# Making the w1 operands of an expert's last group one group earlier, and the gate's Sinkhorn iteration on 128 partitions at fixed places among the products

## The chip, the cores and the metric

The kernel runs on one core of a Trainium2 chip. The metric is the device time of one execution in microseconds (us). A core has five engines that run side by side, each working through its own queue in order: TensorE (PE, matrix products; the load of their stationary operand is shown apart, as PEld), VectorE (DVE), ScalarE (ACT), GpSimd (POOL) and SyncE (SP, which here issues all DMAs). They wait for each other by semaphores. L12 is line 12 of the kernel.

## The reference

```python
attn_out = _attn_ref(**attn_kwargs)            # delta-rule attention, 4 x 8 heads, 768 steps
x = attn_out.transpose(0, 2, 1, 3).reshape(B * S, H * D)      # 3072 tokens x 384
x = _moe_ref(x=x, **moe_kwargs)                # leaky ReLU layer, 384 -> 2048 -> 384
# _moe2_ref
logits = x @ w_gate                            # 3072 x 8
P = np.exp(logits - logits.max())
for _ in range(8):                             # Sinkhorn iteration
    P /= P.sum(1, keepdims=True) + 1e-09
    P /= P.sum(0, keepdims=True) + 1e-09
    P *= N / E
for e in range(E):                             # 8 experts, 384 -> 1024 -> 384
    out += P[:, e:e + 1] * (np.maximum(x @ w1[e], 0.0) @ w2[e])
```

## The kernel before, in words

The program has two parts. Up to about 905 us it computes the attention with the first layer among it, and writes that layer's result x to DRAM. From there to the end it computes the eight experts, and only this second part is touched. Float32 products are made on PE as three passes of split operands: every operand is held as a high part and a low remainder (names ending in h and l), and a product is high x high, high x low and low x high.

**The experts.** The tokens are taken in three blocks p of 1024; for each block the eight experts e run one after the other, 24 in all. An expert has four groups k = 0 to 3 (the list `groups`, L707), and each group makes two of the eight 128-wide slices of the hidden layer. The products of a group follow a Strassen-like scheme of 11 terms (class Group, L894 to L952, in the written order first, second, third, fourth, fifth); each term is three matmuls of 512 columns, issued by `prod` (L872). `second` and `fourth` of a group are issued inside the next group, so that PE always has work. After the fourth group come the products with w2: `second(ps, ...)` (L954) for eight blocks of 128 tokens, eight slices f each, three matmuls of 384 columns per slice; `flush` (L962) adds the block to the accumulator, with the gate's weights pm from expert 1 on, and by a plain ACT copy for expert 0.

**The weights.** `load_w1` and `load_w2` fetch the raw weights of one group by DMA into one of two staging buffers (tile stg, L683). `make_w1(n)` (L727) forms four sums on POOL (L731), then the high part of nine blocks in two ACT instructions (L733, three blocks and six blocks) and the low part in two POOL instructions (L734); `make_w2` is one ACT instruction (L744) and one on POOL (L745). w1 operands live in a ring of three (`w1o[n % 3]`), w2 operands in a ring of five. The queue `prep` (class Stage, L748) holds the tasks: `prep.now()` makes the task at its head and fetches the next loads, so that at most two are staged. The main loop (L981) fills it at k = 0 of each expert and calls `weights()` once per group, inside `fifth` (L949), that is before the group's last three matmuls; three more tasks are made in blocks 1, 3 and 5 of the w2 stage. In the kernel before the order is:

- k = 0: w2 of group n+1; k = 1: w2 of n+2; k = 2: w2 of n+3, then w1 of n+3; k = 3: w2 of n+4
- blocks 1, 3, 5: w1 of n+4, n+5, n+6

Here n is the expert's first group. So w1 of the fourth group (n+3) is made at the end of the third, right before the fourth needs it.

**The order on the engines.** A scheduler orders the instructions of each engine by its own estimate of times. `ordered` (L711) overrides it: it chains an instruction to the one passed to it before on the same engine, so that these keep the written order. Matmuls of the products, the ACT copies and the DVE additions of a group, and the ACT part of the weights are ordered; POOL's instructions, the DMAs, and before the change all of the gate's work are not.

**The gate.** `gate_block` (L564) multiplies 512 tokens with w_gate (six matmuls with 32 stationary columns), transposes on DVE and adds into `logits`, which has 32 partitions x 96 groups x 8 experts. The first five blocks of tokens are done in the first part; the sixth is loaded late (`late_x`, L863, ACT and DVE, not ordered) into tiles of hidden slices 5 to 7, which are free until group 2 of expert 0 writes them. `sinkhorn` (L820) is a generator: each `yield` gives control back until the next call of `bgq.pump`. Before the change `pump` is called once per `prod` and once per block of the w2 stage. It takes the maximum, the exponential, eight iterations of nine DVE instructions with one small matmul (L850, the sum over partitions), and at the end four DMAs (L858) that spread the result over 128 partitions as `pm`. Expert 1's first `flush` needs pm.

Of the kernel before, what the change touches and what calls it, by code (L numbers as in the profile page):

```python
# [8 lines left out]
F32 = mybir.dt.float32  # L9
# [5 lines left out]
ALU = mybir.AluOpType  # L15
# [34 lines left out]
def delta_moe_kernel(ctx: ExitStack, tc: tile.TileContext, k_l, v_l, q_l, beta_l, wa_in, wg, wc, out):  # L50
# [510 lines left out]
            sp.dma_start(out=x2_dram[t, c], in_=o)  # L561


    def gate_block(xh, xl, t, ps_fn, lt):  # L564
        ps = ps_fn()
        for i, x in enumerate((xh, xl)):
            for c in range(KD):
                pe.matmul(out=ps[0:32], lhsT=wg_r[:, c], rhs=x[c] if isinstance(x, list) else x[:, c], start=(i == 0 and c == 0),
                          stop=(i == 1 and c == KD - 1))
            yield  # L570
        dve.transpose(out=lt.rearrange("p g e -> p (g e)"), in_=ps[0:32])
        dve.tensor_tensor(out=logits[:, t * TB // 32:(t + 1) * TB // 32], in0=lt[:, :, 0:E], in1=lt[:, :, E:2 * E],
                          op=ALU.add)
        yield

    if True:
# [238 lines left out]
        def misc(name):  # L815
            return ms_p.tile([128, 512], F32, tag="ms", name=name)

        G = N // 32

        def sinkhorn():  # L820
            yield from gate_block(*g5, NT - 1, lambda: misc("gate"), lt)
            mx = acc_p.tile([32, 1], F32, name="mx")
            dve.tensor_reduce(out=mx, in_=logits, axis=AX.XY, op=ALU.max)
            yield
            ps = misc("mx_ps")
            pe.transpose(out=ps[0:1, 0:32], in_=mx, identity=ident[0:32, 0:32])
            m1 = acc_p.tile([1, 1], F32, name="m1")
            dve.tensor_reduce(out=m1, in_=ps[0:1, 0:32], axis=AX.X, op=ALU.max)
            yield
            ps = misc("mb_ps")  # L830
            pe.matmul(out=ps[0:32, 0:1], lhsT=ones[0:1, 0:32], rhs=m1, start=True, stop=True)
            dve.tensor_copy(out=mx, in_=ps[0:32, 0:1])
            dve.tensor_scalar(out=logits, in0=logits, scalar1=mx, scalar2=None, op0=ALU.subtract)
            p32 = acc_p.tile([32, G, E], F32, name="p32")
            act.activation(out=p32, in_=logits, func=ACTF.Exp)
            yield
            rs = acc_p.tile([32, G], F32, name="rs")
            cs = acc_p.tile([32, E], F32, name="cs")
            for _ in range(8):
                dve.tensor_reduce(out=rs, in_=p32, axis=AX.X, op=ALU.add)  # L840
                dve.tensor_scalar(out=rs, in0=rs, scalar1=1e-9, scalar2=None, op0=ALU.add)
                dve.reciprocal(out=rs, in_=rs)
                dve.tensor_tensor(out=p32, in0=p32, in1=rs.unsqueeze(2).to_broadcast([32, G, E]), op=ALU.mult)
                yield
                dve.tensor_reduce(out=cs, in_=p32.rearrange("p g e -> p e g"), axis=AX.X, op=ALU.add)
                yield
                yield
                yield
                ps = misc("cs_ps")
                pe.matmul(out=ps[0:32, 0:E], lhsT=ones[0:32, 0:32], rhs=cs, start=True, stop=True)  # L850
                yield
                dve.tensor_scalar(out=cs, in0=ps[0:32, 0:E], scalar1=1e-9, scalar2=None, op0=ALU.add)
                dve.reciprocal(out=cs, in_=cs)
                dve.tensor_tensor(out=p32, in0=p32, in1=cs.unsqueeze(1).to_broadcast([32, G, E]), op=ALU.mult)
                dve.tensor_scalar(out=p32, in0=p32, scalar1=float(N // E), scalar2=None, op0=ALU.mult)
                yield
            for k in range(4):
                sp.dma_start(out=pm[32 * k:32 * k + 32], in_=p32.rearrange("p (n k) e -> p k n e", k=4)[:, k])  # L858
            yield

        g5 = [[hb[5 + c][1][i] for c in range(KD)] for i in range(2)]

# [91 lines left out]
        def second(ps, n, blk, fs):  # L954
            o = blk % 4 * 128
            for f in fs:
                w2 = [x[:, f % 2] for x in w2o[(n - n % 4 + f // 2) % W2R]]
                for i, (wt, xx) in enumerate(passes(w2, hb[f][blk // 4])):
                    ordered(pe.matmul(out=ps[:, 0:DM], lhsT=xx[:, o:o + 128], rhs=wt, start=(f == 0 and i == 0),  # L959
                                      stop=(f == NF2 - 1 and i == 2), skip_group_check=True))  # L960

        def flush(ps, p, e, blk):  # L962
            y, a = ps[:, 0:DM], acc[:, blk]
# [12 lines left out]
        def add_w(load, make, n):  # L976
            if n < len(groups):
                prep.add(load, make, n)

        prev = None  # L980
        for n, (p, e, k) in enumerate(groups):  # L981
            g = Group(n)
            if k == 0:
                xs = [2 * p + 2, 2 * p + 3] if e == E - 1 and p < NT // 2 - 1 else []
                for j in range(1, 4):
                    add_w(load_w2, make_w2, n + j)
                add_w(load_w1, make_w1, n + 3)
# [24 lines left out]
            g.hi(0, 1)  # L1012
            second(ps[0], n, 0, range(NF2 - 2))
            g.second()
            g.lo(0, 1)
            g.hi(1, 0)
            g.lo(1, 0)
            second(ps[1], n, 1, range(NF2 - 2))
            g.fourth()
            g.hi(1, 1)  # L1020
            g.lo(1, 1)
            edge = e == E - 1 and p < NT // 2 - 1
            for blk in range(2 * B):
# [12 lines left out]
_OUT = ((N, DM), "float32")  # L1036
# [42 lines left out]
```

## Time and profile before

| | |
|---|---|
| median of 3 runs | 2592.79 us (2587.26 to 2599.87) |
| the profiled execution | 2577.62 us |
| its span, first to last instruction | 2575.9 us |
| mean granted TensorE clock | 0.957 of full speed |
| PE busy | 2401.5 us, 93% of the span |
| PEld, DVE, ACT, POOL busy | 81%, 51%, 45%, 37% |
| the expert part | from about 905 us to the end, 24 experts |

The profile shows one execution. Each row of a timeline gives the start in us from the span's beginning, the length, the engine, the line, the operation and its tiles; in brackets stands how long the engine was idle before it and what released it. A matmul's shown length overlaps the next one, so the distance of two starts is what it costs: about 0.23 us for 512 columns and 0.18 us for 384 at the full clock.

### The profile page before, as it was taken

To read this page: it belongs to the slowest core of one execution; us is meant where nothing else is said; L and a number is where in the kernel's file an instruction comes from. 1 tells how busy PE (TensorE), PEld (TensorE's weight loads), DVE (VectorE), ACT (ScalarE), POOL (GpSimd) and SP (SyncE) were. 2 spreads that over 40 slices of the span, in tenths; PEclk is the share of its full clock that TensorE was granted. 3 is DMA by queue.
4 is the path that set the end of the run, shared out by engine and by line. 5 is a ranking of instruction groups with operands and counts; after the bars stand their busy time and mean duration, and the time that the engine had idled before them with its cause. 6 is when DMAs were issued, how large, how long until landed. Compare 5 with 4: busy or idle time off the path is not lost.

```text
span 2575.9 us, 35446 instructions
## 1 busy us (share of the span) xinstructions
PE 2401.5 (93%) x13836; PEld 2094.3 (81%) x13836; DVE 1302.0 (51%) x2320; ACT 1163.9 (45%) x2121; POOL 964.0 (37%) x966
## 2 busy tenths in 40 slices
PE   6888899999999978999999999999999999999999
PEld 5776778777877767898888888888888888888888
DVE  8667747364622578444444544444444534444443
ACT  6888565756554443333333443333333433333332
POOL 6435211323322223434444444443333434334441
PEclk7678999999999999999999999999999999999999
DMA  3355633333344521111111311111111211111111
GB/s 119 128 171 188 210 130 111 129 103 128 111 150 145 198 68 39 44 49 44 49 44 49 95 48 54 50 44 49 38 49 49 92 50 43 44 49 43 50 43 37
DMA packets 108695, 214.83 MB, mean 83 GB/s; under 512 B 11504, under 2 KB 79728, under 8 KB 108528
## 3 DMA queue, kind: packets, MB, share of 16 engines
q1 hardware_dynamic: 108528, 212.58, 26.4%
q8 instruction: 108, 1.77, 0.3%
q14 instruction: 59, 0.48, 0.1%
HBM read 190.43 MB, written 22.02 MB: 82 GB/s over the span
## 4 chain that ended last, share of the span: by engine, by line
PE 72%; ACT 9%; DVE 7%; issue 5%; POOL 4%; DMA 2%; POOLq 0%; SPq 0%; ACTq 0%; DVEq 0%
PE ye L959 31%; PE ph L875 12%; PE y L875 6%; PE z L875 5%; PE w L875 4%; PE ph L503 4%; PE po L555 4%; ACT x L271 2%; PE y_ps L346 1%; PE w_ps L337 1%; ACT a_d L205 1%; POOL w1l L734 1%; DMA stg<-wc 1%; DVE tm L237 1%; ACT p L287 1%
## 5 line engine op out<-in xcount | busy, mean ns | idle before, releaser
L745 POOL TENSOR_TENSOR w2l<-stg,w2h 128x768 fp32r<-128x768 f32 x96 | 181.6, 1891 | 671.2 <-ACT w2h L744 671.2
L731 POOL TENSOR_TENSOR stg<-stg 128x128 f32<-128x128 f32 x384 | 235.3, 633 | 300.8 <-DMA stg<-wc 293.3
L971 DVE SCALAR_TENSOR_TENSOR acc<-ye,pm,acc 128x384 f32<-128x384 f32 x168 | 103.5, 616 | 437.4 <-PE ye L959 437.4
L734 POOL TENSOR_TENSOR w1l<-stg,w1h 128x384 fp32r<-128x384 f32 x192 | 271.3, 1437 | 56.2 <-ACT w1h L733 35.8
L885 ACT ACTIVATE xc<-ph 128x512 f32<-128x512 f32 x96 | 57.5, 599 | 510.8 <-PE ph L875 408.9
L875 PE MATMUL ph<-xoh,w1l 128*128 128x512 f32 x480 | 197.1, 411 | 42.3 <-POOL w1l L734 42.3
L555 PE MATMUL po<-gh,w 128*128 128x512 f32 (+1 forms) x600 | 215.0, 402 | 2.9 <-ACT gh L543 2.7
L875 PE MATMUL ph<-xoh,w1h 128*128 128x512 f32 x480 | 194.2, 405 | 17.9 <-ACT w1h L733 6.4
L890 DVE TENSOR_TENSOR q<-q,ph 128x512 f32<-128x512 f32 x192 | 131.8, 687 | 119.4 <-PE ph L875 119.4
L875 PE MATMUL ph<-xol,w1h 128*128 128x512 f32 x480 | 188.4, 392 | 0.0
L503 PE MATMUL ph<-x1h,w 128*128 128x512 f32 (+1 forms) x600 | 181.8, 409 | 6.5 <-DVE leak L541 4.0
L733 ACT ACTIVATE w1h<-stg 128x384 fp32r<-128x384 f32 x192 | 121.2, 680 | 117.8 <-DMA stg<-wc 83.7
L890 DVE TENSOR_TENSOR c<-xc,y 128x512 f32<-128x512 f32 x96 | 66.0, 687 | 189.0 <-PE y L875 164.5
L875 PEld LDWEIGHTS ph<-xoh,w1l 128*128 128x128 f32 x480 | 92.6, 193 | 70.9 <-POOL w1l L734 52.3
L541 DVE TENSOR_TENSOR leak<-leak,ph 128x512 f32<-128x512 f32 (+1 forms) x100 | 66.3, 663 | 159.0 <-ACT leak L540 158.6
L875 PEld LDWEIGHTS ph<-xoh,w1h 128*128 128x128 f32 x480 | 93.4, 195 | 51.9 <-ACT w1h L733 16.1
L503 PEld LDWEIGHTS ph<-x1h,w 128*128 128x128 f32 x600 | 110.9, 198 | 29.7 <-DVE leak L541 5.2
L555 PEld LDWEIGHTS po<-gh,w 128*128 128x128 f32 x600 | 113.7, 193 | 25.2 <-ACT gh L543 5.9
L545 POOL TENSOR_TENSOR gl<-leak,gh 128x512 fp32r<-128x512 f32 x48 | 62.1, 1295 | 174.7 <-ACT gh L543 161.8
L555 PE MATMUL po<-gl,w 128*128 128x512 f32 (+1 forms) x300 | 119.4, 399 | 4.7 <-POOL gl L545 3.2
L875 PEld LDWEIGHTS ph<-xol,w1h 128*128 128x128 f32 x480 | 91.0, 190 | 14.9
L540 ACT ACTIVATE leak<-ph 128x512 f32<-128x512 f32 (+1 forms) x100 | 57.8, 578 | 90.0 <-PE ph L503 87.7
(316 smaller groups left out, 6753.2 us busy)
## 6 DMA issues: line engine op xcount, KB each, us to landing
w<-wa_scratch SPq DMA_DIRECT2D x100, 768.0 KB, 4.3
stg<-wc SPq DMA_DIRECT2D x192, 384.0 KB, 3.2
raw<-wa SPq DMA_DIRECT2D x48, 256.0 KB, 3.0
wa_scratch<-cvp SPq DMA_DIRECT2D x48, 256.0 KB, 2.5
stg<-x_scratch SPq DMA_DIRECT2D x10, 768.0 KB, 4.7
q<-q_l SPq DMA_DIRECT2D x24, 256.0 KB, 2.7
v<-v_l SPq DMA_DIRECT2D x24, 192.0 KB, 2.5
x_scratch<-x2o SPq DMA_DIRECT2D x18, 256.0 KB, 3.8
```

The costliest lines, as they stand in the source:

```text
L503: pe.matmul(out=ps, lhsT=wt[:, c * 128:(c + 1) * 128], rhs=xx[:, c], start=(n == 0), stop=(n == 3 * KD - 1))
L541: dve.tensor_tensor(out=g, in0=g, in1=ps, op=ALU.max)
L545: (dve if t in (0, 1, NT - 1) else pool).tensor_tensor(out=gl, in0=g, in1=fr(gh), op=ALU.subtract)
L555: pe.matmul(out=po[c][:, cols], lhsT=wt[:, DM + c * 128:DM + (c + 1) * 128], rhs=xx, start=(i == 1 and m == 0), stop=(i == n and m == 2), ...
L731: pool.tensor_tensor(out=s[:, o], in0=s[:, x], in1=s[:, y], op=op)
L733: ordered(act.activation(out=hi[:, j], in_=s[:, i], func=ACTF.Copy))
L734: pool.tensor_tensor(out=lo[:, j], in0=s[:, i], in1=fr(hi[:, j]), op=ALU.subtract)
L745: pool.tensor_tensor(out=lo, in0=s, in1=fr(hi), op=ALU.subtract)
L875: ordered(pe.matmul(out=ps, lhsT=w[:, a], rhs=x[:, b].rearrange("p s k -> p (s k)"), start=first, stop=i == 2 and (a, b) == terms[-1], ski ...
L890: ordered(dve.tensor_tensor(out=c, in0=x, in1=y, op=op))
L959: ordered(pe.matmul(out=ps[:, 0:DM], lhsT=xx[:, o:o + 128], rhs=wt, start=(f == 0 and i == 0), stop=(f == NF2 - 1 and i == 2), skip_group_ ...
L971: dve.scalar_tensor_tensor(out=a, in0=y, scalar=pm[:, t * B + b, e:e + 1], in1=a, op0=ALU.mult, op1=ALU.add)
```

## The change

The tasks of an expert are queued so that w1 of group n+3 stands second, and `weights()` makes two tasks at k = 1 in place of k = 2. `pump` is called in `second` once per slice f, 64 times per expert, in place of once per block. The Sinkhorn iteration moves its four DMAs to its start (they spread the logits) and works on pm, 128 partitions x 24 groups x 8; all its PE, DVE and ACT instructions and those of its `gate_block` are ordered, that is, they stand in each engine's queue where they are written, with counted pauses between a step and the one that reads it. In the diff, cut to its core, `gate_block` with `ordered` around each instruction is left out.

```diff
-        G = N // 32
+        G = N // 128
...
+        def pause(n):
+            for _ in range(n):
+                yield
...
         def sinkhorn():
-            yield from gate_block(*g5, NT - 1, lambda: misc("gate"), lt)
-            mx = acc_p.tile([32, 1], F32, name="mx")
-            dve.tensor_reduce(out=mx, in_=logits, axis=AX.XY, op=ALU.max)
+            yield from pause(14)
+            yield from gate_block(*g5, NT - 1, lambda: misc("gate"), lt, ordered)
+            for k in range(4):
+                sp.dma_start(out=pm[32 * k:32 * k + 32], in_=logits.rearrange("p (n k) e -> p k n e", k=4)[:, k])
+            yield from pause(6)
+            mx = acc_p.tile([128, 1], F32, name="mx")
+            ordered(dve.tensor_reduce(out=mx, in_=pm, axis=AX.XY, op=ALU.max))
+            yield from pause(2)
+            ps = misc("mx_ps")
+            ordered(pe.transpose(out=ps[0:1, 0:128], in_=mx, identity=ident))
+            yield from pause(2)
...
+            ordered(dve.tensor_copy(out=mx, in_=ps[:, 0:1]))
+            ordered(dve.tensor_scalar(out=pm, in0=pm, scalar1=mx, scalar2=None, op0=ALU.subtract))
             yield
-            act.activation(out=p32, in_=logits, func=ACTF.Exp)
+            ordered(act.activation(out=pm, in_=pm, func=ACTF.Exp))
+            yield from pause(3)
...
             for _ in range(8):
-                dve.tensor_reduce(out=rs, in_=p32, axis=AX.X, op=ALU.add)
+                ordered(dve.tensor_reduce(out=rs, in_=pm, axis=AX.X, op=ALU.add))
...
+                ordered(dve.tensor_reduce(out=cs, in_=pm.rearrange("p g e -> p e g"), axis=AX.X, op=ALU.add))
+                yield from pause(5)
+                ps = misc("cs_ps")
+                ordered(pe.matmul(out=ps[:, 0:E], lhsT=ones, rhs=cs, start=True, stop=True))
+                yield from pause(2)
+                ordered(dve.tensor_scalar(out=cs, in0=ps[:, 0:E], scalar1=1e-9, scalar2=None, op0=ALU.add))
...
-            for k in range(4):
-                sp.dma_start(out=pm[32 * k:32 * k + 32], in_=p32.rearrange("p (n k) e -> p k n e", k=4)[:, k])
-            yield
...
                 for i, (wt, xx) in enumerate(passes(w2, hb[f][blk // 4])):
                     ordered(pe.matmul(out=ps[:, 0:DM], lhsT=xx[:, o:o + 128], rhs=wt, start=(f == 0 and i == 0),
                                       stop=(f == NF2 - 1 and i == 2), skip_group_check=True))
+                bgq.pump(2)
...
-                for j in range(1, 4):
+                add_w(load_w2, make_w2, n + 1)
+                add_w(load_w1, make_w1, n + 3)
+                for j in range(2, 5):
                     add_w(load_w2, make_w2, n + j)
-                add_w(load_w1, make_w1, n + 3)
-                add_w(load_w2, make_w2, n + 4)
...
             def weights():
                 prep.now()
-                if k == 2:
+                if k == 1:
                     prep.now()
...
                 flush(y, p, e, blk)
...
-                bgq.pump(2)
```

## Rows read from the trace of the kernel before

**Rows 1.** Busy time by stretch: us, engines (instructions), PEclk, DMA share, GB/s.
```profile
914.00:982.00 68.00, 54.07 (x252) 45.37 (x251) 62.23 (x88) 26.35 (x44) 26.15 (x26) 0.95 0.19 60
...
1042.33:1110.76 68.43, 66.33 (x325) 59.57 (x325) 29.59 (x44) 23.91 (x40) 28.70 (x29) 0.98 0.17 47
```

**Rows 2.** Chain that ended last, in order of time: the w2 stages of two experts.
```profile
1042.33 27.64 PE ye L959 x156
...
1179.15 27.64 PE ye L959 x156
```

**Rows 3.** Waits of PE: us in total, times, longest.
```profile
PE ph L875 <- POOL w1l L734: 42.3, 23, 2.0
...
PE ph L875 <- ACT w1h L733: 6.4, 23, 0.3
```

**Rows 4.** Timeline of PE around the starts of an expert's third and fourth group.
```profile
1083.20 0.39 PE L875 MATMUL ph<-xoh,w1l 128*128 128x512 f32 x1
...
1086.11 0.39 PE L875 MATMUL ph<-xoh,w1l 128*128 128x512 f32 x1
...
1090.87 0.39 PE L875 MATMUL ph<-xoh,w1l 128*128 128x512 f32 x1
...
1091.54 0.50 PE L875 MATMUL ph<-xoh,w1h 128*128 128x512 f32 x1 [0.28 <-ACT w1h L733]
...
1094.09 0.66 PE L875 MATMUL ph<-xoh,w1l 128*128 128x512 f32 x1 [1.82 <-POOL w1l L734]
...
1097.84 0.39 PE L875 MATMUL ph<-xoh,w1l 128*128 128x512 f32 x1
```

**Rows 5.** Busy time by stretch, right after the wait at 1094 us.
```profile
1095.00:1096.00 1.00, 1.00 (x4) 0.81 (x3) 0.00 (x0) 0.95 (x2) 0.81 (x1) 0.50 0.77 272
```

**Rows 6.** Timeline of POOL in the same groups.
```profile
1083.49 1.85 POOL L745 TENSOR_TENSOR w2l<-stg,w2h 128x768 fp32r<-128x768 f32 x1 [6.12 <-ACT w2h L744]
1088.72 2.58 POOL L731 TENSOR_TENSOR stg<-stg 128x128 f32<-128x128 f32 x4 [3.39 <-DMA stg<-wc]
...
1093.04 2.77 POOL L734 TENSOR_TENSOR w1l<-stg,w1h 128x384 fp32r<-128x384 f32 x2
```

**Rows 7.** Timeline of ACT in the same groups.
```profile
1085.04 0.60 ACT L885 ACTIVATE xc<-ph 128x512 f32<-128x512 f32 x1 [1.63 <-DVE c L890]
...
1090.96 1.25 ACT L733 ACTIVATE w1h<-stg 128x384 fp32r<-128x384 f32 x2
```

**Rows 8.** Timeline of SP: the second and the fourth weight load for the same expert.
```profile
1054.22 0.37 SPq L739 DMA_DIRECT2D stg<-wc  x1
...
1085.36 0.37 SPq L723 DMA_DIRECT2D stg<-wc  x1
```

**Rows 9.** Timeline of PE: group 1 of experts 0 and 2 begins; a wait in expert 0.
```profile
913.77 0.40 PE L875 MATMUL ph<-xoh,w1h 128*128 128x512 f32 x1
...
940.88 0.76 PE L875 MATMUL ph<-xoh,w1h 128*128 128x512 f32 x1 [3.90 <-DVE h31l L904]
...
1075.95 0.39 PE L875 MATMUL ph<-xoh,w1h 128*128 128x512 f32 x1
```

**Rows 10.** Waits of PE, 905 to 1043 us: us in total, times, longest.
```profile
PE cs_ps L850 <- DVE cs L845: 6.7, 6, 2.1
```

**Rows 11.** Instructions of DVE by line, 905 to 1043 us: busy, mean ns, idle before.
```profile
L842 DVE RECIPROCAL rs<-rs 32x96 f32<-32x96 f32 x8 | 5.9, 737 | 0.1
```

**Rows 12.** Timeline of ACT in expert 0.
```profile
916.91 0.63 ACT L691 ACTIVATE h51h<-stg 128x512 fp32r<-128x512 f32 x1 [4.00 <-DMA stg<-x_scratch]
```

**Rows 13.** The four DMAs of line 858: time from issue to landing.
```profile
DMA to landing us min/median/max: 2.2/2.3/2.3
```

**Rows 14.** Timeline of DVE: a low part in expert 0 and one in expert 2.
```profile
936.64 2.03 DVE L904 SCALAR_TENSOR_TENSOR h21l<-c,h21h 128x512 fp32r<-128x512 f32 x1
...
1087.86 0.68 DVE L904 SCALAR_TENSOR_TENSOR h40l<-c,h40h 128x512 fp32r<-128x512 f32 x1
```

**Rows 15.** Timeline of POOL in expert 0.
```profile
936.32 1.81 POOL L745 TENSOR_TENSOR w2l<-stg,w2h 128x768 fp32r<-128x768 f32 x1 [3.51 <-ACT w2h L744]
```

More of the change, by code (lines that the diff above doesn't have):

```diff
@@ L561, in main_a, with gate_block @@
             sp.dma_start(out=x2_dram[t, c], in_=o)
-    def gate_block(xh, xl, t, ps_fn, lt):
+    def gate_block(xh, xl, t, ps_fn, lt, ordered=lambda ins: None):
         ps = ps_fn()
@@ L567, in gate_block @@
             for c in range(KD):
-                pe.matmul(out=ps[0:32], lhsT=wg_r[:, c], rhs=x[c] if isinstance(x, list) else x[:, c], start=(i == 0 and c == 0),
-                          stop=(i == 1 and c == KD - 1))
+                ordered(pe.matmul(out=ps[0:32], lhsT=wg_r[:, c], rhs=x[c] if isinstance(x, list) else x[:, c],
+                                  start=(i == 0 and c == 0), stop=(i == 1 and c == KD - 1)))
             yield
-        dve.transpose(out=lt.rearrange("p g e -> p (g e)"), in_=ps[0:32])
-        dve.tensor_tensor(out=logits[:, t * TB // 32:(t + 1) * TB // 32], in0=lt[:, :, 0:E], in1=lt[:, :, E:2 * E],
-                          op=ALU.add)
+        ordered(dve.transpose(out=lt.rearrange("p g e -> p (g e)"), in_=ps[0:32]))
+        ordered(dve.tensor_tensor(out=logits[:, t * TB // 32:(t + 1) * TB // 32], in0=lt[:, :, 0:E],
+                                  in1=lt[:, :, E:2 * E], op=ALU.add))
         yield
@@ L816, in misc @@
             return ms_p.tile([128, 512], F32, tag="ms", name=name)
-        G = N // 32
+        G = N // 128
+        def pause(n):
+            for _ in range(n):
+                yield
         def sinkhorn():
-            yield from gate_block(*g5, NT - 1, lambda: misc("gate"), lt)
-            mx = acc_p.tile([32, 1], F32, name="mx")
-            dve.tensor_reduce(out=mx, in_=logits, axis=AX.XY, op=ALU.max)
-            yield
[L825 to L828, printed above, removed]
-            yield
[L830 to L834, printed above, removed]
-            act.activation(out=p32, in_=logits, func=ACTF.Exp)
-            yield
-            rs = acc_p.tile([32, G], F32, name="rs")
-            cs = acc_p.tile([32, E], F32, name="cs")
-            for _ in range(8):
-                dve.tensor_reduce(out=rs, in_=p32, axis=AX.X, op=ALU.add)
-                dve.tensor_scalar(out=rs, in0=rs, scalar1=1e-9, scalar2=None, op0=ALU.add)
-                dve.reciprocal(out=rs, in_=rs)
-                dve.tensor_tensor(out=p32, in0=p32, in1=rs.unsqueeze(2).to_broadcast([32, G, E]), op=ALU.mult)
-                yield
[L845 to L856, printed above, removed]
-            for k in range(4):
-                sp.dma_start(out=pm[32 * k:32 * k + 32], in_=p32.rearrange("p (n k) e -> p k n e", k=4)[:, k])
-            yield
@@ new lines, in sinkhorn @@
+            yield from pause(2)
+            m1 = acc_p.tile([1, 1], F32, name="m1")
+            ordered(dve.tensor_reduce(out=m1, in_=ps[0:1, 0:128], axis=AX.X, op=ALU.max))
+            yield from pause(2)
+            ps = misc("mb_ps")
+            ordered(pe.matmul(out=ps[:, 0:1], lhsT=ones[0:1, :], rhs=m1, start=True, stop=True))
+            yield from pause(2)
+            ordered(dve.tensor_copy(out=mx, in_=ps[:, 0:1]))
+            ordered(dve.tensor_scalar(out=pm, in0=pm, scalar1=mx, scalar2=None, op0=ALU.subtract))
@@ new lines, in sinkhorn @@
+            yield
+            ordered(act.activation(out=pm, in_=pm, func=ACTF.Exp))
+            yield from pause(3)
+            rs = acc_p.tile([128, G], F32, name="rs")
+            cs = acc_p.tile([128, E], F32, name="cs")
+            for _ in range(8):
+                ordered(dve.tensor_reduce(out=rs, in_=pm, axis=AX.X, op=ALU.add))
+                ordered(dve.tensor_scalar(out=rs, in0=rs, scalar1=1e-9, scalar2=None, op0=ALU.add))
+                ordered(dve.reciprocal(out=rs, in_=rs))
+                ordered(dve.tensor_tensor(out=pm, in0=pm, in1=rs.unsqueeze(2).to_broadcast([128, G, E]), op=ALU.mult))
+                ordered(dve.tensor_reduce(out=cs, in_=pm.rearrange("p g e -> p e g"), axis=AX.X, op=ALU.add))
+                yield from pause(5)
+                ps = misc("cs_ps")
+                ordered(pe.matmul(out=ps[:, 0:E], lhsT=ones, rhs=cs, start=True, stop=True))
+                yield from pause(2)
+                ordered(dve.tensor_scalar(out=cs, in0=ps[:, 0:E], scalar1=1e-9, scalar2=None, op0=ALU.add))
+                ordered(dve.reciprocal(out=cs, in_=cs))
+                ordered(dve.tensor_tensor(out=pm, in0=pm, in1=cs.unsqueeze(1).to_broadcast([128, G, E]), op=ALU.mult))
+                ordered(dve.tensor_scalar(out=pm, in0=pm, scalar1=float(N // E), scalar2=None, op0=ALU.mult))
+                yield
```

## The prediction

> **What bounds the kernel now.** I read the busy times by stretch first. One expert, from its w2 stage to that of the next, takes 68.43 us, and PE is busy in 66.3 us of it, while DVE, ACT and POOL are busy for less than 30 us each [rows 1]. So the expert part is bound by PE, and only PE's own idle time or slow time can be won. The chain of waits repeats the same stage at that period [rows 2]. The list of PE's waits then shows what is left to win: 42.3 us in 23 waits for the low part of w1 (POOL, L734) and 6.4 us in 23 waits for its high part (ACT, L733), 48.7 us or 2.12 us for each of 23 experts [rows 3]. Expert 0 is not among them, as other waits hide its own.
>
> The timeline of PE shows what such a wait costs beyond its length. From the last matmul of group 1 (1083.20) to the last of the twelfth after it (1086.11) PE takes 2.91 us; the same twelve matmuls behind group 2 take 6.97 us, 1090.87 to 1097.84 [rows 4]. The difference is 4.06 us, of which 0.28 and 1.82 us are the two waits. The rest, 1.9 us, is the clock: in the microsecond after the wait the granted clock is 0.50, the 1.2 GHz level, with PE busy all through it [rows 5]. Only the fourth group starts like this; the third, whose w1 was made an expert earlier, starts without.
>
> **Part 1, the order of the weights.** The cause of the wait is read on POOL: after the low part of w2 the low part of w1 begins at 1093.04, when PE has already run dry [rows 6]. The change makes this w1 one group earlier. The products that last read its place in the ring (group 0's `fourth`) are issued before that point, so no new wait for the place arises.
>
> What moves, engine by engine. ACT gets 1.25 us of high parts ahead of group 2's first copy instead of group 3's; that copy now waits 1.63 us for DVE with ACT idle [rows 7], so 0.38 us of slack stays and I cost it at nothing. Without that cover it would cost up to 1.25 us per expert. POOL gets 2.77 us of low parts ahead of the low part of w2, which ran from 1083.49 to 1085.34 [rows 6] and now ends near 1083.1 + 2.77 + 1.85 = 1087.7 us, or a little later where the second high part is late. That w2 is needed only in the w2 stage, 15 us on. The four sums (2.58 us, [rows 6]) go where POOL is idle, ahead of the expert. On SP w1's load takes the place of the second load, issued at 1054.22, more than 25 us before ACT needs it [rows 8]; w2 of n+2 and n+3 come one staging turn later. The fourth load would follow the end of w1's low parts at about 1086 us, a little after its present 1085.36 [rows 8]; it needs some 3.4 us to POOL's first use [rows 6] and its ACT instruction stands at 1090.2 (w1h's start of 1090.96 less a w2h): close, but in time, and ACT has the idle time above behind it.
>
> With w1 ready, the fourth group should start as the third does now. That gives 23 x 4.06 = 93.4 us. Bounds: if the waits go but the clock still falls, only 48.7 us; nothing in the rows allows more.
>
> **Part 2, the gate.** Expert 0 and 1 hold all of it. From group 1 of expert 0 (913.77, [rows 9]) to the end of expert 1's w2 stage (1042.33 + 27.64 = 1069.97, [rows 2]) PE needs 156.2 us. The same products two experts later, 1075.95 to 1206.79 [rows 2, 9], take 130.8 us. These hold two of the w1 waits, so without them 122.7 us. Part 1 already counts expert 1's wait, so 156.2 - 4.1 - 122.7 = 29.4 us are what the gate costs now. DVE is why: it is busy 62.2 of 68 us in expert 0 against 29.6 in a later one [rows 1], and PE waits for it, 6.7 us at the small matmul of the iteration [rows 10] and 3.9 us at the fourth group's start, with a slow stretch behind it [rows 9].
>
> After the change each DVE instruction of the iteration reads a quarter of the elements per partition. The reciprocal of 96 takes 737 ns [rows 11]; for 24 I take 0.3 us, between a quarter of it and all of it, and for the nine instructions of an iteration 2.5 us where 6.3 us stood. Where do they fall? `pump` is called 32 times in the products of an expert and 64 times in the w2 stage. Counting the pauses, the first iteration begins at call 36, the w2 stage at call 31, and the iteration ends at call 100, in expert 1's first group, ahead of the first use of pm. So all eight iterations lie in expert 0's w2 stage, where `flush` is on ACT and DVE has little else. Eight calls are 24 matmuls of 27.64 / 156 = 0.177 us [rows 2], 4.25 us for an iteration of 2.5 us: hidden, and the small matmul comes five calls (2.7 us) after the DVE chain began.
>
> What is not hidden stays as cost: (a) six gate matmuls on PE at 0.23 us, 1.4 us, as before; (b) eight small matmuls, now with 128 stationary columns, and three more around the maximum: between nothing and two matmuls of 512 columns each, I take 4 us in all; (c) the late load of x, for which ACT sat 4.00 us [rows 12] with the first copies queued behind it: PE's gate matmuls no longer stand in front, but the copies do, 1.5 us (0 to 4); (d) expert 0's own w1 of group 3, whose load has to wait for the late x to leave its staging buffer, some 2.5 us after ACT begins on it at 916.91 [rows 12], and needs 3.4 us of transfer and 2.6 us of sums [rows 6], so that ACT is held until about 925.5 us: a wait of 2 us with its slow stretch, 3.7 us (0 to 6); (e) the maximum, ordered on DVE six calls after the four DMAs, each 2.3 us to landing [rows 13] and queued on SP among weight loads: 2.5 us (0 to 8). These are 13.1 us of the 29.4, so 16 us are gained; with the ends of each between 7 and 25.
>
> **The sum.** 93.4 + 16.3 = 109.7 us. Against the profiled execution's 2577.6 us this gives 2468; the median of the runs lies 15.2 us above that execution, and I set the forecast against the median: 2592.8 - 109.7 = 2483 us.
>
> **The rivals.**
> *The low parts block each other.* POOL's 1.85 us of w2l now ends near 1087.7, and DVE's first low part of group 2 starts at 1087.86 [rows 14]. In expert 0 a low part that started inside a w2l of 1.81 us took 2.03 us and not 0.68 [rows 14, 15]. If POOL runs a little later than I think, each expert's DVE loses up to 1.35 us there; the fourth group's first matmuls write a bank that DVE reads last, so PE would wait as long at the old place, and the slow clock with it: 1.35 + 1.9 us in 23 experts, 75 us of the 109.7 given back, 2558 us. For it speaks the small margin; against it that the sums no longer run beside DVE's low parts of group 2. The Trainium skill (SBUF — State Buffer, section Who interferes with whom) says that a DVE instruction with two SBUF inputs and a GpSimd instruction that reads SBUF exclude each other for the whole instruction; the 2.03 us agree, the low part having waited for w2l's end. Chance 0.08.
> *The clock is not given back.* If the slow stretch came for another reason than the wait, only 48.7 + 16.3 = 65 us are won: 2528 us. Against it: the third group's start has no wait and no slow stretch [rows 4]. Chance 0.06.
> *Nothing moves.* If the scheduler set POOL's unordered w1 work behind other work, or something else is late at the same place, part 1 gives nothing and part 2 its 16 us: 2577 us. Chance 0.04.
> *Slower than before.* ACT's high parts of w1 are ordered, so if their data are late, ACT stops with every copy of group 2 behind it. It decides when the load is issued: if a staging buffer came free only with w2 of n+1 (the third load instead of the second), the path is 3.4 us of transfer, 2.6 us of sums and 1.25 us of high parts after it, 7.25 us, less the idle 1.63 us [rows 6, 7]; with 1.9 us of slow clock that is 7.5 us in each of 23 experts, 173 us lost against the 109.7 gained: 2656 us. Beyond 4.8 us per expert it turns the sign. Against it: the second load is issued at 1054.22, long before [rows 8]. Chance 0.02.
>
> **How the numbers follow.** My forecast has 0.80: 2483 us, its own range 2466 to 2505 (part 2 between 7 and 25 us, some 7 us for the spread of runs, and up to 7 us for small overlaps of POOL and DVE). To reach 8 in 10 the range takes in the case of the clock up to 2530 us; the blocked, the unmoved and the slower case are left out. A measurement of this kernel tells about 0.5% (13 us) from no change. Faster by more than that: the forecast and the first two rivals and about half of the third, 0.95; within it 0.03; slower 0.02.
>
> **What would show it.** In the changed profile the waits of PE for L734 and L733 are gone or a few us; the period of an expert is near 64.4 us; the granted clock stays at full in the first products of the fourth group; w1's high parts stand on ACT before group 2's first copy without a wait for DMA or POOL. Two experts from group 1 of expert 0 to the end of expert 1's w2 stage take near 136 us, and no row of the iteration stands among DVE's waits in the products. I am wrong if DVE's low parts become long in group 2, if PE waits for DVE or ACT at the fourth group's start, or if the maximum or the late x hold PE for more than some 10 us.

## The result and the profile after

The changed kernel takes 2483.49 us (median of 3 runs, 2483.44 to 2491.82) against 2592.79 us: a ratio of 0.9587, 95% interval 0.9539 to 0.9635. The forecast was 2483 us, a gain of 109.7 us; measured are 109.3 us. The profiled execution itself took 2491.82 us, 85.8 us less than the profiled one of before, not 109. The expert part accounts for more than that, the untouched first part for the rest with the other sign, so the reading goes by stretches of the expert part.

Two rows of the chain that ended last, in order of time, bound the later experts: the w2 stage of expert 1 and that of the last expert, 22 experts on. They answer to [rows 2].

```profile
1045.72 27.55 PE ye L964 x156
...
2458.79 27.57 PE ye L964 x156
```

(2458.79 - 1045.72) / 22 = 64.23 us for an expert. Before it was (2544.83 - 1042.33) / 22 = 68.30 us. The busy times by stretch, for one expert (us, then PE, PEld, DVE, ACT, POOL busy with instructions, granted clock, DMA share, GB/s), answer to [rows 1]:

```profile
1045.72:1109.97 64.25, 64.25 (x326) 58.38 (x325) 28.38 (x44) 23.91 (x40) 26.68 (x29) 1.00 0.18 50
```

PE is busy in all of it and the clock is at full, where it stood at 0.98 with 2.1 us idle. The timeline of PE at the third and the fourth group answers to [rows 4]:

```profile
1094.19 0.39 PE L880 MATMUL ph<-xoh,w1l 128*128 128x512 f32 x1
1094.44 0.50 PE L880 MATMUL ph<-xoh,w1h 128*128 128x512 f32 x1
...
1097.08 0.39 PE L880 MATMUL ph<-xoh,w1l 128*128 128x512 f32 x1
```

From the end of the third group to the twelfth matmul after it are 2.89 us where 6.97 stood, and the fourth group starts like the third. In the list of PE's waits no entry is left from 1073 us to the end. On POOL, ACT and DVE the order came out as worked out; the first two fences are timelines of POOL and ACT (to [rows 6, 7]), the third is DVE's first low part of the third group (to [rows 14]).

```profile
1086.49 2.83 POOL L734 TENSOR_TENSOR w1l<-stg,w1h 128x384 fp32r<-128x384 f32 x2 [5.80 <-ACT w1h L733]
1089.28 1.85 POOL L745 TENSOR_TENSOR w2l<-stg,w2h 128x768 fp32r<-128x768 f32 x1
```
```profile
1085.88 1.26 ACT L733 ACTIVATE w1h<-stg 128x384 fp32r<-128x384 f32 x2
1087.03 0.85 ACT L744 ACTIVATE w2h<-stg 128x768 fp32r<-128x768 f32 x1
1088.36 0.60 ACT L890 ACTIVATE xc<-ph 128x512 f32<-128x512 f32 x1 [0.47 <-DVE c L895]
```
```profile
1091.18 0.68 DVE L909 SCALAR_TENSOR_TENSOR h40l<-c,h40h 128x512 fp32r<-128x512 f32 x1
```

ACT's idle time ahead of the copy shrank from 1.63 to 0.47 us and was not used up. POOL's low part of w2 ends at 1091.13, 0.05 us before DVE's low part starts.

In experts 0 and 1 the stretch of the prediction, from group 1 of expert 0 to the end of expert 1's w2 stage, is 936.50 to 1073.27, 136.8 us, where 156.2 stood and 136 was forecast. PE's waits from 926 to 1074 us (us in total, times, longest) answer to [rows 10]:

```profile
PE ph L880 <- DVE q L895: 3.1, 1, 3.1
PE cs_ps L858 <- DVE cs L855: 2.6, 3, 1.0
PE ph L880 <- DVE c L895: 1.3, 1, 1.3
PE ph L880 <- ACT xc L890: 0.2, 1, 0.2
```

So the whole expert part, from group 1 of expert 0 to the end of the span, went from 2575.9 - 913.77 = 1662.1 us to 2489.8 - 936.50 = 1553.3 us: 108.8 us. Of these, 22 x 4.07 = 89.5 lie in experts 2 to 23 and 19.4 in the stretch. In the stretch lay expert 1's own wait for w1, and this one was not worth 4.1 us, as the prediction took it, but its length alone, 2.1 (0.28 and 1.82 us). PE's timeline before shows it:

```profile
1026.97 0.50 PE L875 MATMUL ph<-xoh,w1l 128*128 128x512 f32 x1 [1.82 <-POOL w1l L734]
...
1029.12 0.39 PE L875 MATMUL ph<-xoh,w1l 128*128 128x512 f32 x1
```

The nine matmuls from the one to the other take 2.15 us, at the full clock; the same nine behind expert 2's wait, 1094.09 to 1097.84 in [rows 4], take 3.75. In each of the 22 later experts the matmuls behind the wait are slow, behind expert 1's none is. So the gate's share of the 19.4 us is 17.3.

Up to group 1 of expert 0, where every engine's queue is the same, the changed kernel's profile is 22.7 us longer (936.50 against 913.77); the last section returns to that.

All runs below are read by the same marks: the start of group 1 of expert 0, the start of the 156-matmul run in expert 1's w2 stage, the same of the last expert.

| kernel | group 1 of expert 0 | expert 1's run | stretch, us | last run | period, us |
|---|---|---|---|---|---|
| before | 913.77 | 1042.33 | 156.2 | 2544.83 | 68.30 |
| changed | 936.50 | 1045.72 | 136.8 | 2458.79 | 64.23 |
| e1 weights only | 930.55 | 1056.17 | 153.3 | 2471.80 | 64.35 |
| e2 gate only | 919.18 | 1034.51 | 142.9 | 2536.60 | 68.28 |
| e3 w1 first in the third group | 934.31 | 1041.39 | 134.6 | 2461.72 | 64.56 |
| e4 w2 first in the second group | 918.17 | 1027.86 | 137.2 | 2441.41 | 64.25 |
| e5 gate not ordered | 932.53 | 1039.86 | 134.9 | 2452.99 | 64.23 |
| e6 gate on 32 partitions, ordered | 938.01 | 1067.91 | 157.6 | 2483.39 | 64.34 |
| e7 late x later | 926.11 | 1037.53 | 139.0 | 2450.62 | 64.23 |
| e8 low part twice | 924.83 | 1036.82 | 139.5 | 2480.71 | 65.63 |
| e9 low part three times | 924.41 | 1045.57 | 148.7 | 2596.63 | 70.50 |
| e10 not ordered, expert 0's w1 late | 929.35 | 1036.36 | 134.6 | 2449.22 | 64.22 |
| e11 changed again | 920.45 | 1030.72 | 137.8 | 2443.52 | 64.22 |

The stretch is the second mark plus the run's length (27.55 to 27.65 us) less the first; the period is the distance of the two runs over 22. The first mark leaves out a wait of PE for ACT in expert 0's first group, 0 to 2.3 us long in these profiles. Counted from expert 0's first product, the changed kernel takes 146.0 us in its first profile and 148.5 in its second (e11), so a difference of 2 us between two stretches says little.

### The profile page after: what moved, and what is told of

It is laid out like the page before. It is cut to its first block, busy times and chain, and to the rows that moved or that the text cites. A ratio compares the mean times of both kernels' runs of the same rounds, so it can differ in the third digit from the quotient of the medians.

```text
span 2489.8 us, 35427 instructions
## 1 busy us (share of the span) xinstructions
PE 2374.4 (95%) x13836; PEld 2087.3 (84%) x13836; DVE 1263.4 (51%) x2320; ACT 1162.8 (47%) x2121; POOL 937.5 (38%) x966
## 4 chain that ended last, share of the span: by engine, by line
PE 77%; ACT 10%; DVE 7%; issue 3%; DMA 2%; POOL 2%; SPq 0%; ACTq 0%; POOLq 0%; DVEq 0%
PE ye L964 32%; PE ph L880 13%; PE w L880 5%; PE y L880 5%; PE z L880 5%; PE ph L503 4%; PE po L555 4%; PE y_ps L346 2%; ACT x L271 2%; PE w_ps L337 2%; ACT a_d L205 1%; ACT p L287 1%; PE g_ps L189 1%; ACT u L297 1%; DVE tm L237 1%
## 5 line engine op out<-in xcount | busy, mean ns | idle before, releaser
L731 POOL TENSOR_TENSOR stg<-stg 128x128 f32<-128x128 f32 x384 | 209.0, 565 | 305.5 <-DMA stg<-wc 284.5
L880 PE MATMUL ph<-xoh,w1l 128*128 128x512 f32 x480 | 188.1, 392 | 0.0
```

The lines of the kernel that those rows point to most:

```text
L731: pool.tensor_tensor(out=s[:, o], in0=s[:, x], in1=s[:, y], op=op)
L880: ordered(pe.matmul(out=ps, lhsT=w[:, a], rhs=x[:, b].rearrange("p s k -> p (s k)"), start=first, stop=i == 2 and (a, b) == terms[-1], ski ...
```

## The experiments

**Each part alone.** e1 is the kernel before with the new order of the tasks only:

```diff
-                for j in range(1, 4):
+                add_w(load_w2, make_w2, n + 1)
+                add_w(load_w1, make_w1, n + 3)
+                for j in range(2, 5):
                     add_w(load_w2, make_w2, n + j)
-                add_w(load_w1, make_w1, n + 3)
-                add_w(load_w2, make_w2, n + 4)
...
-                if k == 2:
+                if k == 1:
```

> Part 1 alone: the new order of the weight tasks, the gate as before. My theory (the wait for w1 and the slow clock behind it are 4.06 us in each of 23 experts): period of a late expert 64.3 us, about 93 us less than before, ratio about 0.964; experts 0 and 1 stay near 156 us less 4 from group 1 of expert 0 to the end of expert 1's w2 stage. Rival (the two parts need each other, DVE's load from the gate or the pump in the w2 stage matter for the later experts): the period stays above 66 us, ratio above 0.98.

It took 2506.93 us, ratio 0.9662 (0.9617 to 0.9708) to the kernel before, which took 2595.77 us beside it. The period is 64.35 us, all but 0.1 us of the changed kernel's. The stretch stays long, 153.3 us: it lost 2.9 us and not 4, nearer to the 2.1 us of expert 1's wait alone. The small matmul still waits for DVE (waits of PE, us in total, times, longest):

```profile
PE cs_ps L850 <- DVE cs L845: 8.2, 6, 3.0
PE ph L875 <- DVE h31l L904: 2.9, 1, 2.9
```

e2 is the changed kernel with these lines undone.

> Part 2 alone: the gate on 128 partitions at written places, the weight tasks in the old order. My theory: 15 us less than before and nothing in the later experts, period 68.3 us, ratio about 0.994, which the times can hardly tell from no change, while the trace shows it between group 1 of expert 0 and the end of expert 1's w2 stage (137 to 145 us, as expert 0 and 1 now show their own wait for w1, where before took 156). Rival (the gate was hidden and its 25 us are clock alone): the same stretch stays within 5 us of 156 us.

It took 2579.29 us, ratio 0.9937 (0.9914 to 0.996), so the gain could be told from no change after all. The period is that of before; the stretch fell by 13.3 us to 142.9. The waits for w1 are back, and now expert 0 has one too, 24 in place of 23:

```profile
PE ph L880 <- POOL w1l L734: 44.0, 24, 2.0
PE ph L880 <- ACT w1h L733: 6.7, 24, 0.3
```

The two parts do not need each other. Their gains by the trace nearly add up: 22 x 3.95 + 2.9 = 89.8 us and 13.3 us, plus expert 0's own wait that e2 uncovers (1.71 and 0.28 us at 944.70, at the full clock behind it), is 105 of the 108.8. The rest, some 4 us, was not traced; two profiles of the changed kernel differ by 2.5 us.

**Where w1 is made, and in which order.** e3 makes w1 of the last group in the third group as before the change, but ahead of that group's w2:

```diff
                 add_w(load_w2, make_w2, n + 1)
-                add_w(load_w1, make_w1, n + 3)
-                for j in range(2, 5):
-                    add_w(load_w2, make_w2, n + j)
+                add_w(load_w2, make_w2, n + 2)
+                add_w(load_w1, make_w1, n + 3)
+                add_w(load_w2, make_w2, n + 3)
+                add_w(load_w2, make_w2, n + 4)
...
-                if k == 1:
+                if k == 2:
```

> The changed kernel, with w1 of the last group made in the third group again, but ahead of that group's w2 instead of behind it. My theory (the wait was the length of the w2 low part that stood in front on POOL, 1.8 us, and the slow clock came with the wait): ACT's first high part starts 0.85 us earlier and the low part 1.8 to 2.5 us earlier, so that the wait falls from 2.1 us to under 0.5 us in each expert, the clock stays at full, period 64.3 to 65 us, ratio to the kernel before 0.958 to 0.966. Rival (w1 has to be made a group earlier to be in time, the clock falls after any wait there): period 66.5 to 68 us, ratio above 0.98.

2492.38 us, ratio 0.9604 (0.9569 to 0.964), period 64.56 us. POOL's timeline shows the swap: the low part of w1 first, that of w2 behind it; the matmul that reads the first low part starts at 1090.89 with no wait listed.

```profile
1089.82 2.82 POOL L734 TENSOR_TENSOR w1l<-stg,w1h 128x384 fp32r<-128x384 f32 x2 [5.38 <-ACT w1h L733]
...
1092.60 1.86 POOL L745 TENSOR_TENSOR w2l<-stg,w2h 128x768 fp32r<-128x768 f32 x1
```

So w1 did not have to be made a group earlier. What made it late was the w2 ahead of it on ACT and POOL; taking it out of the way gives 3.74 of the 4.07 us. The swap also moves w1's load and its sums one place forward, but these were not what POOL waited for last: before, the four sums ended at 1091.30 [rows 6], and what filled POOL from there to the low part at 1093.04 was the low part of w2. The group earlier gives the last 0.33 us and the margin.

e4 makes both in the second group, w2 first, which was meant to put w1's low parts beside DVE's low parts. It has e3's lines of `add_w`, with `k == 1` kept.

> The changed kernel, with the two tasks of the second group in the other order: w2 of n+2, then w1 of n+3. So w1's load is the third of the expert and its low parts run on POOL some 2 us later, beside DVE's first low parts of the third group. The rival of the prediction (POOL and DVE block each other there, and PE waits for DVE at the start of the fourth group): low parts on DVE of 1.0 to 2.0 us instead of 0.68, a wait of PE for DVE of 0.5 to 1.4 us in each expert, period 65 to 67.5 us, ratio to the kernel before 0.97 to 0.99. My theory for the changed kernel holds in either case; if DVE has slack enough, the period stays at 64.3 us and the ratio at 0.958.

2483.32 us, ratio 0.9581 (0.9537 to 0.9625), period 64.25 us: no loss. DVE's timeline has the only low part of that expert's third group that got longer, by 0.15 us, and not by the 0.3 to 1.3 us expected: POOL's pair of low parts of w1, 2.83 us from 1070.75, ended at 1073.58, so the two overlapped for 0.28 us only.

```profile
1073.30 0.83 DVE L909 SCALAR_TENSOR_TENSOR h40l<-c,h40h 128x512 fp32r<-128x512 f32 x1
```

So a small overlap costs nothing. The long one that the prediction's first rival feared did not come about here, and what it would cost stays untested.

**What a wait costs.** e8 and e9 take e3 and write the first low part (three blocks, about 1 us) of each expert's last w1 two and three times:

```diff
-                pool.tensor_tensor(out=lo[:, j], in0=s[:, i], in1=fr(hi[:, j]), op=ALU.subtract)
+                for _ in range(2 if n % 4 == 3 and j.start == 0 else 1):
+                    pool.tensor_tensor(out=lo[:, j], in0=s[:, i], in1=fr(hi[:, j]), op=ALU.subtract)
```

> The kernel with w1 made first in the third group (period 64.56 us, low part just in time), with the first low part of w1 of each expert's last group written twice: 1.0 us more on POOL in front of PE, so a wait of about 1.1 us in each expert. If a wait costs its length, the period becomes 65.6 us. If a wait of this length also brings the slow clock, as the one of 2.1 us did, 67.5 us.

2512.76 us, ratio 0.9694 (0.9658 to 0.9731). The wait of PE, and the microsecond behind one of them (busy times by stretch; the granted clock is the number after POOL's):

```profile
PE ph L881 <- POOL w1l L735: 25.5, 24, 1.1
```
```profile
1088.00:1089.00 1.00, 1.00 (x6) 0.83 (x5) 0.00 (x0) 0.75 (x2) 1.00 (x1) 1.00 0.09 25
```

The wait is 25.5 / 24 = 1.06 us and the period grew by 65.63 - 64.56 = 1.07 us. Here a wait of this length costs its length; no matmul behind any of the 24 waits is slow.

> The same with that low part written three times: 2.0 us more, a wait of about 2.1 us in each expert, as long as in the kernel before. If the slow stretch there belonged to the wait, the period comes back to 68.3 to 68.6 us and the granted clock falls to half behind each wait. If it belonged to something else in the old order, the period is 66.6 us with the clock at full.

2626.7 us, ratio 1.014 (1.01 to 1.018): slower than before. The size was missed: the scheduler put the third writing behind the six-block low part, so the wait was 90.5 / 24 = 3.77 us, not 2.1. The period grew by 70.50 - 64.56 = 5.94 us, 2.17 us more than the wait, and the clock behind it is at half:

```profile
PE ph L881 <- POOL w1l L735: 90.5, 24, 3.8
```
```profile
1100.00:1101.00 1.00, 1.00 (x4) 0.81 (x3) 0.00 (x0) 0.95 (x2) 0.60 (x1) 0.50 0.76 175
```

With the kernel before that makes three sizes at one place: 1.06 us of wait cost 0.01 us beyond itself, 2.10 us cost 1.9 in 22 of 23 experts and nothing in expert 1, and 3.77 us cost 2.2 on average, with 5 to 13 slow matmuls behind each of its 24 waits. So the slow stretch comes with the wait, not in proportion to it, and at 2.10 us not every time.

**What brings the gate's gain.** e5 keeps the 128 partitions and the pauses, but orders none of the gate's instructions:

```diff
+        def placed(ins):
+            return ins
...
-                ordered(dve.tensor_reduce(out=rs, in_=pm, axis=AX.X, op=ALU.add))
+                placed(dve.tensor_reduce(out=rs, in_=pm, axis=AX.X, op=ALU.add))
...
```

> The changed kernel, but the gate's instructions are not ordered: 128 partitions and the pauses stay, the scheduler places them by its own estimate. If the smaller DVE work alone brings the gain of part 2: from group 1 of expert 0 to the end of expert 1's w2 stage 135 to 139 us, as in the changed kernel. If the written places matter: more than 141 us, with waits of PE for the small matmul or for DVE among the products. The time as a whole within 1% of the changed kernel in both cases (ratio to the kernel before 0.955 to 0.965).

2471.23 us, ratio 0.953 (0.9487 to 0.9573); the stretch is 134.9 us, 1.9 us shorter than the changed kernel's, with 3.3 us of waits at the small matmul and one of 1.9 us for DVE. Both the ratio and the stretch lie just below what was expected. Of the 12 to 14 us by which its median is below the changed kernel's two, the profile shows 2 in the expert part (2484.0 - 932.53 = 1551.5 us against 1553.3); where the rest lies was not traced.

e6 does the reverse: the iteration on 32 partitions as before, ordered at the same places, the DMAs at its end.

```diff
-        G = N // 128
+        G = N // 32
...
-            rs = acc_p.tile([128, G], F32, name="rs")
+            rs = acc_p.tile([32, G], F32, name="rs")
...
-                ordered(pe.matmul(out=ps[:, 0:E], lhsT=ones, rhs=cs, start=True, stop=True))
+                ordered(pe.matmul(out=ps[0:32, 0:E], lhsT=ones[0:32, 0:32], rhs=cs, start=True, stop=True))
```

> The changed kernel with the iteration on 32 partitions again, its instructions ordered at the same pauses, and the four DMAs behind it. One iteration's DVE chain is then 6.3 us against 4.25 us of products between its places, so if the length of the chain is what counts, PE waits 2 us and more at each of the eight small matmuls, and the stretch from group 1 of expert 0 to the end of expert 1's w2 stage takes 150 to 160 us. If the written places bring the gain, it stays at 136 to 142 us.

2509.47 us, ratio 0.9668 (0.9632 to 0.9703); the stretch is 157.6 us, 4.3 us longer than in e1, which has the same weights and the gate as before. All eight small matmuls wait for the chain:

```profile
PE cs_ps L857 <- DVE cs L854: 14.6, 8, 2.7
```

The gain of part 2 is the shorter chain on DVE. The order adds nothing to it: without it the gain stays (e5), and on 32 partitions it makes things worse (e6). The pauses and the calls of `pump` per slice are in both versions, so what they do by themselves is not shown.

**Two attempts at the rest.** e7 splits the late x one group later, ordered behind group 1's first copies:

```diff
         def late_x(t, s):
             for c in range(KD):
-                parts(g5[0][c], g5[1][c], s[:, c], dve)
+                ordered(act.activation(out=g5[0][c], in_=s[:, c], func=ACTF.Copy))
+            for c in range(KD):
+                ordered(dve.tensor_tensor(out=g5[1][c], in0=s[:, c], in1=fr(g5[0][c]), op=ALU.subtract))
...
-        prep.now()
+        prep.fetch()
...
             g.first(prev)
+            if n == 1:
+                prep.now()
...
             def weights():
+                if n == 0:
+                    return prep.fetch()
+                if n == 1:
+                    prep.now()
                 prep.now()
```

> The changed kernel with the late load of x split on ACT and DVE one group later, ordered behind the first copies of group 1 of expert 0, and the weight tasks of groups 0 and 1 made together. If the 3.1 us wait of PE for DVE there, with its slow stretch, is ACT sitting in front of the late x: that wait goes or falls under 1 us, and the stretch from the first product of expert 0 to the end of expert 1's w2 stage gets 3 to 5 us shorter; the time as a whole changes by less than the runs scatter (0 to -5 us against the changed kernel). If the wait has another cause, or the weights made later cost as much, the stretch stays within 1 us.

2488.63 us, ratio 0.9594 (0.9557 to 0.963). The stretch from group 1 grew to 139.0 us. From expert 0's first product on it takes 1065.08 - 916.89 = 148.2 us, against 146.0 in the changed kernel's first profile and 148.5 in its second. The timeline of PE shows why: the wait only shrank, and a second one came up a group later.

```profile
932.89 0.50 PE L882 MATMUL ph<-xoh,w1h 128*128 128x512 f32 x1 [2.52 <-DVE q L897]
...
946.21 0.50 PE L882 MATMUL ph<-xoh,w1h 128*128 128x512 f32 x1 [2.54 <-DVE q L897]
```

What made these two waits is read on DVE and on ACT:

```profile
930.34 0.69 DVE L872 TENSOR_TENSOR h51l<-stg,h51h 128x512 fp32r<-128x512 f32 x1 [1.22 <-ACT h51h L870]
```
```profile
942.58 0.85 ACT L744 ACTIVATE w2h<-stg 128x768 fp32r<-128x768 f32 x1 [4.16 <-DMA stg<-wc]
```

The copies of group 1 were now on time, but the low parts of the late x, ordered on DVE by this very edit, waited for ACT and stood in front of the addition that PE waits for (932.15). A group later ACT stood 4.16 us on the load of a w2 that had become late. So the edit took ACT's wait away and put two others in its place, and it does not show what the late x alone costs.

e10 joins e5 with e3's order for expert 0 alone (`k == (2 if n < 4 else 1)`); e11 is the changed kernel again.

> The two readings put together: the gate on 128 partitions without the written places, and in expert 0 alone w1 of the last group made in the third group, ahead of its w2, so that ACT does not sit in front of its load in the second. From group 1 of expert 0 to the end of expert 1's w2 stage 131 to 134.5 us, where the changed kernel took 136.8; the rest as in the changed kernel (period 64.2 us). The time 2 to 5 us below the changed kernel's, less than single runs scatter.

> The changed kernel once more, beside the version above on the same chip: ratio to the kernel before 0.957 to 0.961, stretch 136 to 138 us, period 64.2 us; the start of group 1 of expert 0 anywhere between 914 and 938 us, as in the profiles so far.

e10: 2479.44 us, ratio 0.9569 (0.9539 to 0.9599), stretch 134.6 us, just outside what was expected, and no shorter than e5's 134.9 within what two profiles of one kernel differ. e11: 2485.15 us, ratio 0.9589 (0.9553 to 0.9624), stretch 137.8 us. By the stretch e10 is 2 to 3 us better than the changed kernel (1 to 3 us from expert 0's first product, 145.2); by the times the two can't be told apart.

## Why the prediction was right

**The bound and part 1.** PE bound the experts, and in experts 2 to 23 a wait for w1 with the slow clock behind it was worth 4.06 us: the period fell by 4.07 us. e1 shows that this holds without the gate's part. The price was read at one expert and taken for all 23; expert 1's wait had no slow clock behind it and was worth 2.1. So part 1 is 22 x 4.07 + 2.1 = 91.6 us and not 93.4, and the gate's cost before, worked out by taking 4.1 us off, was 31.4 and not 29.4. In the total the two slips cancel. That the clock comes back with the wait was the second rival's point; e8 and e9 show it by making that wait longer at the same place. The cause was named as POOL's order, w1 behind w2, which e3 shows. The slack on ACT (0.38 us worked out, 0.47 read) and the end of POOL's w2 (1087.7 against a low part at 1087.86, read as 1091.13 against 1091.18) came out as written, and so no new wait appeared. Of the rival in which POOL and DVE block each other, the changed kernel shows only that POOL ended 0.05 us before DVE's low part began, and e4 that an overlap of 0.28 us costs nothing.

**Part 2.** 16.3 us were forecast and 17.3 measured; left over are 136.8 - 122.7 = 14.1 us where 13.1 were forecast. The sum held partly by luck: three terms came out some 7 us dearer, and two, set at 6.2 us, cost nothing.

- (a), the six gate matmuls, cost their 1.4 us.
- (b), the small matmuls, were set at 4 us. The matmuls around the eleven stand some 6 us further apart than elsewhere, 2.6 of them waits. The waits come from three iterations in which DVE was blocked (below). The 128 stationary columns are not the reason: around one that does not wait, as at 972.25, PE loses 0.2 us.
- (c), the late x, was set at 1.5 us and is the largest miss. ACT sits on its DMA as before, and the copies behind it are late (timelines of ACT and of PE):

```profile
939.59 0.63 ACT L691 ACTIVATE h51h<-stg 128x512 fp32r<-128x512 f32 x1 [3.94 <-DMA stg<-x_scratch]
...
941.90 0.57 ACT L890 ACTIVATE xc<-ph 128x512 f32<-128x512 f32 x1
```
```profile
943.85 0.50 PE L880 MATMUL ph<-xoh,w1h 128*128 128x512 f32 x1 [3.09 <-DVE q L895]
```

From 936.50 to group 2's first matmul at 949.01 PE issues 33 matmuls of 0.23 us, 7.6 us, in 12.5: 4.9 us lost, the wait and the slow stretch behind it.

- (d), expert 0's own w1, was set at 3.7 us and cost nothing that the waits show: by the delay of (c) its load and sums were there in time (w1's high parts ran at 947.38 and 948.05, 0.03 us after the sums had ended). e10, which takes (d) away, gained at most 0.3 us over e5.
- (e), the maximum behind four DMAs, was set at 2.5 us and cost nothing: the DMAs were issued at 953.76 and the maximum ran at 959.35 with no wait before it.
- One term was missing. The prediction's count of calls let the last iteration end in expert 1's first group, yet it went on to put all eight into expert 0's w2 stage. The eighth ended at 1012.54, in expert 1, and expert 1's eight scalings of the accumulator (L976), which need pm, followed at once on DVE. Four of them stood in front of a group's additions, and PE waited 1.3 us (the wait for DVE c in the list of waits above):

```profile
1012.57 2.99 DVE L976 TENSOR_SCALAR acc<-acc,pm 128x384 f32<-128x384 f32 x4
```

With 1.4 us of (a), some 6 of (b) and 4.9 of (c) that makes 13.6 of the 14.1 us. The chain of an iteration was set at 2.5 us on DVE. Undisturbed it is 0.35 + 0.18 + 0.30 + 0.36 + 0.52 + 0.17 + 0.20 + 0.36 + 0.26 = 2.7 us. The ends given for part 2, 7 and 25 us, do not follow from the terms: their ends add up to 1.4 and 24.5 us, which makes 5 and 28. The measured gain lies inside both.

One step of the reasoning was not needed. The prediction counted the calls of `pump` to show that the iteration falls into expert 0's w2 stage, as if the places were part of the gain. e5 does without the order and loses nothing, e6 has the order and gains nothing.

**The number.** The forecast was set against the median of the runs and hit it within a microsecond. That is luck: single runs of one kernel scatter over 5 to 25 us. The two profiled executions alone would have shown 85.8 us.

## What to carry to other kernels

A wait of the bounding engine that repeats is priced by two like stretches of its timeline, one with the wait and one without, because the clock behind it can cost as much again; the wait list alone would have given half of this gain. Price more than one occurrence: here 22 of 23 had the slow clock behind them. Before work is moved a whole stage earlier, look at what stands in front of it in the same queue: here a swap of two neighbours (e3) gives over nine tenths of it. And where a small iteration sits on an engine that the main loop needs, shorten its instructions first (here by spreading it over all partitions); where they are placed came second.

## What the runs showed of the hardware that was not expected

**A half clock behind some waits of 2 us and not behind others.** At one place, the start of the fourth group, 1.06 us of idle PE had only matmuls at the full clock behind them, in all 24 experts (e8; the granted clock shown is 1.00), and 3.77 us had slow ones, in all 24 (e9; 0.50, the 1.2 GHz level). Waits of 2.10 us in the kernel before were followed by slow matmuls in experts 2 to 23, at a cost of about 2 us each, and by a granted clock of 1.00 in expert 1. In its expert 0, too, waits of 2.52 us (917.60) and 2.41 us (928.65) had only matmuls at the full clock behind them. So the length of a wait does not settle it; what else does was not tried.

**DVE held up by POOL with one input in SBUF.** In the changed kernel the iteration's last scaling (L863, one tensor by a constant) takes 0.26 us, and 1.79 us when POOL writes a low part of w1; the timelines of DVE and of POOL:

```profile
983.76 0.26 DVE L863 TENSOR_SCALAR pm<-pm 128x192 f32<-128x192 f32 x1
...
988.97 1.79 DVE L863 TENSOR_SCALAR pm<-pm 128x192 f32<-128x192 f32 x1
```
```profile
987.71 2.94 POOL L734 TENSOR_TENSOR w1l<-stg,w1h 128x384 fp32r<-128x384 f32 x2 [1.86 <-ACT w1h L733]
```

It ends at 990.76, after POOL's pair of instructions at 990.65. The instruction before it (L862, two inputs in SBUF), at 987.82 beside the first of the pair, took 1.12 us and not 0.36. The same happened at 978.79 and 999.15, and these are the chains that PE waited for. The prediction had looked for this among the low parts only. The Trainium skill (SBUF — State Buffer, section Who interferes with whom) counts such a scaling by a constant among the instructions that can take the port pair shared with GpSimd, and says that whoever comes second waits for the whole instruction; these rows agree.

**A first part that scatters.** Up to group 1 of expert 0 all kernels issue the same instructions, and the mark lies anywhere from 913.77 to 938.01 us in 13 profiles. In the kernel before (the first row) the granted clock from 300 to 600 us is 0.99, in e6 (the second) 0.94:

```profile
300.00:600.00 300.00, 279.58 (x2128) 230.18 (x2128) 169.54 (x388) 180.36 (x325) 73.82 (x69) 0.99 0.41 135
```
```profile
300.00:600.00 300.00, 282.38 (x2098) 235.24 (x2098) 168.74 (x388) 174.93 (x317) 68.80 (x64) 0.94 0.39 130
```

In that time the trace of the one with the lower clock has 30 matmuls less of the same list, and 8 instructions less on ACT. That goes with the clock; what sets it off in one execution and not in another was not tried.
